# Gated mix of a state-space convolution and a routed feed-forward: parameter products ahead of the transposition, wide products, and cross-block sums by accumulating transfers

## The chip, the cores and the metric

The kernel runs on one core of one Trainium2 chip. The metric is the device time of one execution in microseconds; the time before is the median of 2 runs. Each execution can leave a profile; times inside it are counted from the start of its span.

## The reference

Input x = `A_u` has 2048 tokens of 512 channels. The output is a gated mix of two branches:

```
g   = sigmoid((x * gate_w).sum(-1))                    # per token
# branch a: state-space convolution, per channel d
A, B, C = complex (512, 128);  dt = exp(log_dt)
K[d,l]  = Re sum_n C[d,n] * exp(dt[d]*A[d,n]*l) * dt[d]*B[d,n]      # l < 2048
a   = irfft(rfft(pad(x)) * rfft(pad(K)))[:2048] + x * Dskip         # length 4096, along tokens
# branch b: the two tokens with the largest r = x @ w_r go through a feed-forward
y   = (silu(x_sel @ w_gate) * (x_sel @ w_up)) @ w_down * sigmoid(r_sel)
b   = x with y added at those two tokens
out = g * a + (1 - g) * b
```

## The kernel before, in words

The 512 channels are two halves h = 0, 1 of 256, the 2048 tokens two blocks of 1024. Every step is entered by `Prog.op` with the engine, the buffers it reads and writes and a cost; a step that may run on ACT or on DVE is given both. The order is not left to a planner at run time: the string ORDER lists all steps in the order in which each engine gets them, and SECOND says by one digit for each step whether it takes the first or the second engine named. `emit` then puts a semaphore wait ahead of a step for what it needs from another engine. So each engine works its own list in strict order, and a step that waits holds up all that stands behind it in that list. Transfers are issued by SP, or by ACT where a step says so. Most operations are entered through helpers, so their line in the profile is that of the helper: L483 is a product or sum of two tensors on DVE, L494 a function on ACT, L498 an eviction (PSUM to SBUF, on either engine), L502 a scaling for the arguments of sine and cosine, L505 a DMA.

The stages:

1. *Parameters.* A_re, A_im, C_re, C_im, B_re, B_im (four blocks of 128 channels x 128 states each) are loaded. dt is spread over the partitions by a matmul (L621) and exponentiated. 24 PE transposes (L628) bring all six to states x channels. DVE then forms AL = dt·A_re, the angle B16 from dt·A_im (L648, L651), PBR = dt·B, CM1 and CM2 (the products with C_re and C_im), and from these WW = C·B·dt in the channel order of the kernel (four small sums).
2. *Exponentials and angle tables.* 26 exponentials of AL multiples on ACT, arguments (L502, L694) on DVE or ACT, sine and cosine on ACT. The function sets of ACT differ, so a switch loads a table (L255 and the first at L494). DVE multiplies exponentials, sines and earlier tables into the rows r0 to r3 for each half (r0h to r3h; r31 is the last of half 1).
3. *Routing and feed-forward* on PE with small steps elsewhere (logits L771, gather L812, edge tokens `xed` L820, feed-forward L835, L851), and the transform of the input on PE (L900), whose evictions fill X (named x<h><block> here).
4. *kgen(h)*: 256 narrow matmuls (L917) make the kernel K of one half from the tables, evicted to KA (ka). Small selections (L933 to L966) and, for half 1, twenty small transfers on SP within SBUF (`tap`) arrange it as KC.
5. *kspec(h)*: matmuls with 128 KB spectrum matrices (L986, KP) and a cross term (L991) make the kernel's spectrum, evicted to KK (kk): for block i, real or imaginary part, quarter qd, even or odd.
6. *products(h, qds, blks)*: complex products of X and KK on DVE. Block 1 of the output needs X of block 1 with KK of block 0 plus X of block 0 with KK of block 1, so there are two further products and two additions. For block 1 of half 0 before, this is done quarter pair by quarter pair (`qd` 0, then 1), each in its own buffers PQ; block 0 is done in one wide pass in PM.
7. *inverse(h)*: per block, matmuls add the token-wise parts (`fin`, L1038, L1039) and the inverse transform with G (L1051); evictions L1059 scale by the gate into U, and a DMA writes 128 KB of output.

In the list before, half of kspec(0) (quarter pair 0) stands ahead of kgen(1) on PE and half behind it; DVE's list has products of half 0 while kgen(1) runs.

Of the kernel before, what the change touches and what calls it, by code (L numbers as in the profile page):

```python
# [58 lines left out]
class Prog:  # L59
# [47 lines left out]
    def schedule(self):  # L107
# [15 lines left out]
        dma_free = {SP: 0.0, ACT: 0.0}  # L123
# [250 lines left out]
ETB = sorted({tok(s)[0] for _, _, src in EROWS for s in src})  # L374
# [4 lines left out]
def small_mats():  # L379
    eye = np.eye(128)  # L380
    sgn = np.diag(np.where(np.arange(128) % 2 == 0, 1.0, -1.0))
    xs = np.zeros((128, len(ETB), EW))
    ek = np.zeros((128, 4, 2, EW))
    oh = np.zeros((NE, 16 * 128))
    for r, (t, k, src) in enumerate(EROWS):
        for s in src:
            tb, p = tok(s)
            xs[p, ETB.index(tb), 32 + r] = 1.0
# [4 lines left out]
    return np.concatenate([eye, sgn, -sgn, xs.reshape(128, -1), ek.reshape(128, -1)], 1), oh  # L393
# [3 lines left out]
    "00100300p00q00r00200000700o01401500601700501801c01b01p00402201e00h01d01601i01y01f01k01v01g00g01901q01j01h01x01a00802301u03u04w01n01o03t02s00a04x03v00s"  # L397
    "00t00u00v02002402d01r04303s04404200w00x00y00z01002b01s01t00c02604500901101201l01301w02102702q05903w03x03z04603y02t04704805b04z04y01m05805a04902g04005c"
    "00b02j04f05005105204a04104b05d05f02502m02i05e02u05g05h05302902o02r05502n05402p02v04n01z04e02w02l04c02a00e03304m05s03404d00i02k03502c05t03602f02e04p037"
    "03802h04g05600f02805v04o04q03903a04j05u03b03i05700d04h05w04t04i04r04s04k03d05i05k03j07807907a04l05j05l00n07l03o07s07j07b07c05y00l04u05m07r07i03e03f07t"  # L400
    "07k07m00j07e07h07q07d07u06004v07n05x05z06105n05p07g03g07o05o05q07v06207w03k03l09s06307f07p09t09h06e06f09r07x03m05r06h03n03q09u09v06g09i06506407y06609w"
    "06i06709x09j07z08108006j08309k06k06m0680820ae08508409l06906l06n08609m09o06b06a06c06d09n08908b0ad08a08e08f0a408h06z09y08c0a308808706y07003p06o08d0a1071"
    "07200k08g08i08j0ac09p0a20a508k08l08m08o08n08q0ab09z0af0a808p06q08s08r0a609q0a70a006p0a900m06r0am0al0ag08t0aa0an08u0ao07408w0b80ai0ah0ay0ax0az0ap0b508v"
    "0aj0b708y08x0aw0900b60ak08z0920au0aq0ar0at03r02x07306s06u0b00b306w0av0b90b106t0ba0bb0bc0as0be0bh0bd0b20b40bf0760bg0bj0bi0750bl0910bk0bu09306v0br09d0bq"
    "09c0bm0bp09409e0bt0bw0bs0bn0770950980bo0bv09609709a09f0c80bx09g02y0990ca06x0du0cb0c60c70c40cf0cl0cm03002z0310320er0ex0ey0cg0c50cc0by0c90f60cd0cn0f50bz"
    "0ch0f00ci0cj0ck09b0d80d90da0db0dc0ce0f70dd0de0df0f80dg0dh0di0dk0dj0dl0dm0do0dn0dq03h0dp0ds0dt03c0ei0co0f40dr0e20cp0e40f90eu0fa0fc0es0ec0fb0fe0cq0cr0ej"
    "0cs0ez0ev0ew0ct0cu0cv0c00cw0f20cx0f30cy0ff0e70d20c10e30cz0d00d10d30d40fg0eq0fd0c20c30f10d50d60ep0d70eg0fh0e90eh0fi0ek0em0en0e10el0h20h60gz0h10fj0fk0h0"
    "0dx0e60fl0ee0fm0dw0h30h50fn0h40eb0fo0ha0dy0fp0eo0hd0dv0ed0h70fq0he0hf0hp0hb0ef0h80h90hg0hn0hc0et0ho0hh0hi0hq0e50e00dz0fs0e80ea0fv0g10g20fw0fr0ft0fx0fy"
    "0fz0g60gc0g00fu0g30g70g40g50hu0gd0g80g90ga0gb0gh0gi0hj0gf0ib0gj0ge0ic0id0gg0gn0i40ie0gl0if0hr0gk0gq0gm0gr0gs0gw0go0gt0gp0hk0gu0ht0i50gv0ig0ii0ih0im0il"
    "0in0gx0gy0i10hv0i20ik0i30hs0hy0hz0i60ia0hw0jf0ij0jj0jg0i00hl0je0hx0i70jd0jk0jh0io0ip0iq0ir0is0iu0ju0it0jl0jm0jv0jn0ji0jo0iw0jw0iv0iy0jp0jq0ix0iz0i80j1"  # L410
    "0j20j30j00j70jr0js0jz0k10jt0k20k50j40j60jy0j50j80j90k30k70k40ja0jb0i90jc0k60ka0kb0k90kd0ke0kf0k00kg0kj0kk0kh0k80ki0kl0jx0kc0km0kp0hm0kq0kn0ko0kr0ks"
)
SECOND = (
    "000000000000000000000000000000000000000000000000000110000000000000000000000000000000000000000000000000000000000000000000000000000000000001110001001110"
    "000100011001010010110001001100000000010000100001000000000000000000001100000000000000000000000000000000000000001100000000001000001001000000000000000000"
    "000000000000000000000000000000000000000000000010000000101010001000001001100010100110000000000111010001101000000000000000000000000000000000000000001000"
    "000000000100000000000000000000000000000000000000000000000000000000000000000100001101100110100100000000000000000000000000000000000000000000000000000000"
    "00000000000000000000000010000110000000000000000000000000000000000000000000000000000000000000000000000000000000000000000000000000000000010110010000000"
# [5 lines left out]
def bass_gated_mix__ssm_conv_s4__moe_arch_mod__prompt_kernel(nc, A_u, A_A_re, A_A_im, A_B_re, A_B_im, A_C_re, A_C_im, A_log_dt, A_Dskip,  # L424
# [22 lines left out]
    with ExitStack() as es:  # L447
# [73 lines left out]
        CF = B("cf", oS, 640, F32); RTS = B("rts", oS + 640, 1280, F32);  # L521
# [10 lines left out]
        PBR = B("pbr", oX, 4 * KB, F32)  # L532
# [555 lines left out]
        for qd in range(2):  # L1088
            products(0, (qd,), (1,), pset=qd)
# [57 lines left out]
```

## Time and profile before

| what | us |
|---|---|
| median of 2 runs | 169.3 (169.01 to 169.58) |
| the profiled execution's own time | 168.23 |
| its span in the profile | 166.4 |
| last sine on ACT ends | 79.9 |
| last table row (r31) ends on DVE | 92.86 |
| kgen(1) on PE | 92.92 to 102.2 |
| last product ends on DVE | 159.33 |
| last output DMA issued | 164.30 |

The profiled execution is 1.83 us longer than its span; what lies around the span is not seen by the profile. Busy time is given for PE (matmul), PEld (weight load), DVE, ACT and POOL; a busy share of an engine is an average over stages, so the stages are read one by one. In the chain of waits each row is a start, a duration and the work; consecutive rows follow from what released what. In the groups of instructions, the mean is one instruction's own duration; back to back they start some 0.08 us closer than that.

### The profile page before, as it was taken

Reading aid. Unit: us, or ns where it says so; the run is one execution under the profiler, and the core shown is the slowest. Engines: PE = TensorE matmul, PEld = TensorE weight load, DVE = VectorE, ACT = ScalarE, POOL = GpSimd, SP = SyncE. Lnnn points to the kernel's source line nnn. Section 1 sums busy time; section 2 is a strip of 40 time slices with the busy share of each in tenths; the row PEclk is TensorE's granted clock in tenths of the full one; section 3 lists DMA queues with packets and bytes.
Section 4 is the critical chain, followed back from the end, with each engine's and each line's share of the span. In section 5 each row is a group of like instructions: output and inputs, shape, how many; then the busy total and the mean of one; then the engine's idle time right before and its main releaser. Section 6 shows DMA issues by size and latency. Waiting matters only on the chain.

```text
span 166.4 us, 3916 instructions
## 1 busy us (share of the span) xinstructions
PE 148.1 (89%) x1644; PEld 101.7 (61%) x1644; DVE 152.9 (92%) x255; ACT 117.2 (70%) x197; POOL 2.8 (2%) x7
## 2 busy tenths in 40 slices
PE   5999959999999998997489999968989999989980
PEld 1644415456364348692257799837857888878860
DVE  1699998899999998999999999999999999999970
ACT  3499999799999999999744777992043658408022
POOL 2000000000000000000000004000000000000000
PEclk9999987999999999999858999999999999999999
DMA  4999998996000000000995502941020000130505
GB/s 151 218 341 203 146 241 290 415 398 267 4 0 0 0 4 0 4 0 7 330 353 196 190 7 61 378 123 26 13 61 8 0 0 0 35 95 0 158 4 160
DMA packets 22584, 20.33 MB, mean 122 GB/s; under 512 B 12187, under 2 KB 19102, under 8 KB 22438
## 3 DMA queue, kind: packets, MB, share of 16 engines
q1 hardware_dynamic: 22276, 19.81, 39.7%
q8 instruction: 13, 0.21, 0.5%
q10 hardware_dynamic: 290, 0.26, 0.5%
q14 instruction: 5, 0.04, 0.1%
HBM read 15.54 MB, written 2.10 MB: 106 GB/s over the span
## 4 chain that ended last, share of the span: by engine, by line
DVE 52%; ACT 28%; PE 9%; issue 6%; DMA 2%; SPq 0%; DVEq 0%
DVE AR L483 44%; ACT AR L494 13%; ACT AR L498 7%; ACT AR L502 4%; PE ps L900 3%; ACT AR L694 3%; DVE AR L498 2%; PE ps L1051 2%; PE ps L628 2%; DVE AR L502 2%; DMA AR<-c_bf 2%; DVE AR L880 1%; PE ps L917 1%; PE ps L771 1%; DVE AR L1059 1%
## 5 line engine op out<-in xcount | busy, mean ns | idle before, releaser
L483 DVE TENSOR_TENSOR AR<-AR 128x1024 bf16<-128x1024 bf16 (+8 forms) x151 | 119.9, 839 | 1.3
L498 ACT ACTIVATE AR<-ps 128x512 bf16<-128x512 f32 (+7 forms) x71 | 45.0, 667 | 17.9 <-PE ps L986 10.2
L900 PE MATMUL ps<-AR 128*128 128x512 bf16 x192 | 45.5, 390 | 2.4 <-DVE AR L498 2.1
L494 ACT ACTIVATE AR<-AR 128x512 bf16<-128x512 f32 (+4 forms) x56 | 41.4, 791 | 2.6 <-DVE AR L483 2.2
L900 PEld LDWEIGHTS ps<-AR 128*128 128x128 bf16 x192 | 18.1, 100 | 25.4 <-DVE AR L498 2.6
L1051 PE MATMUL ps<-AR 128*128 128x256 bf16 x256 | 30.4, 273 | 1.3 <-DVE AR L483 1.3
L1051 PEld LDWEIGHTS ps<-AR 128*128 128x128 bf16 x256 | 24.8, 98 | 5.1 <-DVE AR L483 1.9
L1059 ACT ACTIVATE AR<-ps,AR 128x256 bf16<-128x256 f32 x25 | 10.8, 474 | 21.9 <-PE ps L1051 21.7
L986 PE MATMUL ps<-AR 128*128 128x256 bf16 x160 | 21.0, 282 | 0.3 <-issue 0.3
L917 PEld LDWEIGHTS ps<-AR 128*128 128x128 bf16 x512 | 18.8, 98 | 2.1 <-ACT AR L498 0.7
L917 PE MATMUL ps<-AR 128*128 128x84 bf16 (+1 forms) x512 | 19.4, 199 | 0.5 <-ACT AR L498 0.4
L986 PEld LDWEIGHTS ps<-AR 128*128 128x128 bf16 x160 | 15.5, 101 | 4.5 <-issue 0.7
L502 DVE TENSOR_SCALAR AR<-AR 128x256 int32<-128x256 f32 (+1 forms) x39 | 11.4, 325 | 0.6 <-ACT AR L494 0.6
L502 ACT ACTIVATE AR<-AR 128x256 int32<-128x256 f32 (+1 forms) x25 | 10.0, 437 | 0.0
L617 PE MATMUL ps<-AR 128*128 128x512 bf16 x28 | 8.3, 462 | 1.5 <-DVE AR L612 1.5
L1038 PE MATMUL ps<-AR 128*128 128x256 bf16 x32 | 7.7, 274 | 2.1 <-DVE AR L498 1.4
L1039 PE MATMUL ps<-AR 128*128 128x256 bf16 x32 | 7.6, 273 | 0.0
L483 DVE TENSOR_TENSOR AR<-AR,ps 128x256 f32<-128x256 bf16 (+2 forms) x6 | 3.4, 627 | 4.1 <-PE ps L628 4.1
L617 PEld LDWEIGHTS ps<-AR 128*128 128x128 bf16 x28 | 3.0, 112 | 5.4 <-issue 1.9
L991 PE MATMUL ps<-AR 128*128 128x512 bf16 x16 | 5.6, 380 | 0.1
L694 DVE TENSOR_SCALAR AR<-AR 128x1024 int32<-128x1024 int32 (+1 forms) x9 | 5.7, 629 | 0.0
L1038 PEld LDWEIGHTS ps<-AR 128*128 128x128 bf16 x32 | 3.1, 97 | 3.6 <-DVE AR L498 1.5
(66 smaller groups left out, 81.6 us busy)
## 6 DMA issues: line engine op xcount, KB each, us to landing
AR<-c_ksp SPq DMA_DIRECT2D x5, 512.0 KB, 5.5
AR<-c_inv SPq DMA_DIRECT2D x1, 2048.0 KB, 8.0
out_dram<-AR SPq DMA_DIRECT2D x16, 128.0 KB, 2.2
AR<-in_B_w_gate_dram SPq DMA_DIRECT2D x1, 1792.0 KB, 12.8
AR<-in_B_w_up_dram SPq DMA_DIRECT2D x2, 896.0 KB, 10.9
AR<-c_fwd SPq DMA_DIRECT2D x3, 512.0 KB, 6.9
AR<-in_A_u_dram SPq DMA_DIRECT2D x2, 512.0 KB, 5.3
AR<-in_A_u_dram SPq DMA_DIRECT2D x1, 1024.0 KB, 7.7
```

The lines of the kernel that those rows point to most:

```text
L483: return P.op(DVE, lambda h: h.tensor_tensor(out=o, in0=a, in1=b, op=op), rd, wr, cost=tt_cost(o, a, b), **k)
L494: return P.op(ACT, lambda h: h.activation(out=o, in_=a, func=func, scale=scale, bias=bias), rd, wr, cost=0.185 + nel(o) * 0.833e-3 + (0.09 ...
L498: return P.op((ACT, DVE), (lambda h: h.activation(out=o, in_=a, func=ACTF.Copy), lambda h: h.tensor_copy(o, a)), rd, wr, cost=(0.185 + n * ...
L502: return P.op((ACT, DVE), (lambda h: h.activation(out=o, in_=a, func=ACTF.Copy, scale=c), lambda h: h.tensor_scalar(out=o, in0=a, scalar1= ...
L617: last = h.matmul(fwp[1](0, 128, k * 512, (1, D)), DUM(0, 128, 0, (1, 128)), DUM(0, 128, 0, (1, D)), start=True, stop=True)
L694: P.op((DVE, ACT), (lambda hh: hh.tensor_scalar(out=w, in0=w, scalar1=16384.0, scalar2=None, op0=ALU.add), lambda hh: hh.activation(out=w, ...
L900: last = h.matmul(o, w, U2(0, 128, st * D, (1, D)) if pm else U(0, 128, (blk * 8 + st * 2 + par) * D, (1, D)), start=(pm + par + st == 0), ...
L917: last = hh.matmul(pb(0, 128, (g - b0) * W4 + o, (1, n)), TP[h][1 - i // 2](0, 128, g * 128, (1, 128)), r[i](0, 128, g * n, (1, n)), start ...
L986: last = hh.matmul(pb(0, 128, n * 256, (1, 256)), KP[u](0, 128, (tau + n) * 128, (1, 128)), KC[h](0, 128, jg * 256, (1, 256)), start=(k == ...
L1038: hh.matmul(pb(0, 128, e * 256, (1, 256)), IDN(0, (1, 128)), U(0, 128, tb[e] * D + h * HC, (1, HC)), start=(e == 0), stop=False)
L1051: last = hh.matmul(pb(0, 128, e * 256, (1, 256)), G(0, 128, ((par * 2 + part) * 4 + ft) * 512 + (2 * t2 + e) * 128, (1, 128)), X(0, 128, h ...
L1059: P.op((ACT, DVE), (lambda hh, o=o, i_=i_, g_=g_: hh.activation(out=o, in_=i_, func=ACTF.Copy, scale=g_), lambda hh, o=o, i_=i_, g_=g_: hh ...
```

## The change

- *Parameters.* A_re and A_im alone are brought over by 8 matmuls with a permuted identity, so they come out in the kernel's channel order at once; dt is spread in that order too. C and B are multiplied on DVE in their natural layout (PAB, bf16), and 16 accumulating matmuls (identity and negated identity NID) both transpose the products and add them up to C·B; WW is one product with dt. B_im is issued on ACT behind the exponential of dt in ACT's list.
- *Edge tokens.* Two row loads bring the few token rows (XSR), and one matmul with a selection matrix takes the place of four.
- *Taps of half 1.* Every second one is issued by ACT. The load of G stands behind the SP ones.
- *Block 1 of half 0* is one pass over both quarter pairs. Its two cross products go to PT and to X's own block-1 place, and are added to PM by POOL: two groups, each of two DMAs of 128 x 2048 bf16 with `accum_op=ADD`.
- *Outputs* are grouped by pairs of token tiles of the same parity; still 16 of 128 KB.
- *Order.* New ORDER and SECOND: all 26 exponentials come before the first sine; all of kspec(0) stands behind kgen(1) on PE; in DVE's list, four ka evictions of half 1, eight kk evictions of half 0 and two wide products come between r31 and the first cross product; then u scalings, kc1's addition, the second cross product, eleven steps of half 1 (kk1 evictions and products of quarter pair 0), and behind them the subtraction that needs both accumulated buffers. DVE takes more evictions than before, ACT fewer. kspec(1) stands ahead of inverse(0).

```diff
-        dtp = kgp[1]
-        pps = [misb[0], misb[1], kgb[0]]
...
-                        last = h.transpose(pps[q](0, 128, i * D + k * 128, (1, 128)), PRM(0, 128, (2 * q + i) * D + k * 128, (1, 128)), IDN(0, (1, 128)))
+        TS(NID(0, 128, 0, (1, 128)), IDN(0, (1, 128)), -1.0, ALU.mult, [CBI], [NID])
...
+                    last = h.matmul(pto(psa[q], 0, k), PRM(0, 128, q * D + k * 128, (1, 128)), idp(CB, 0), start=True, stop=True)
+        for q in range(2):
+            TT(PAB(0, 128, q * 1024, (D, 2), (1, D)), PRM(0, 128, 2 * D, (D, 2), (1, D)), PRM(0, 128, (4 + q) * D, (0, 2), (1, D)), ALU.mult, [(PRM, 2), (PRM, 3), (PRM, 4 + q)], [(PAB, q)])
+        for part in range(2):
+            def pwr(h, part=part):
+                for k in range(4):
+                    h.matmul(pto(psw, part * D, k), PAB(0, 128, part * D + k * 128, (1, 128)), idp(CB, 0), start=True, stop=False)
+                    last = h.matmul(pto(psw, part * D, k), PAB(0, 128, 1024 + (1 - part) * D + k * 128, (1, 128)), idp(CB, 0) if part else idp(NID, 0), start=False, stop=True)
...
+        TT(f512(AL), f512(DTB), psa[0](0, 128, 0, (1, D)), ALU.mult, [DTB, psa[0].buf], [AL])
+        STT(f512(TMP[1]), psa[1](0, 128, 0, (1, D)), -c16, f512(DTB), ALU.mult, ALU.mult, [DTB, psa[1].buf], [TMP[1]])
...
-        TT(PBR(0, 128, 0, (D, 2), (128, 4), (1, 128)), DTB(0, 128, 0, (0, 2), (1, 4), (4, 128)), pps[2](0, 128, 0, (D, 2), (128, 4), (1, 128)), ALU.mult, [DTB, pps[2].buf], [PBR])
-        TT(c2(CM1), pps[1](0, 128, 0, (D, 2), (1, D)), PBR(0, 128, 0, (0, 2), (1, D)), ALU.mult, [pps[1].buf, PBR], [CM1])
-        TT(c2(CM2), pps[1](0, 128, 0, (D, 2), (1, D)), PBR(0, 128, D, (0, 2), (1, D)), ALU.mult, [pps[1].buf, PBR], [CM2])
-        for h_ in range(2):
-            TT(prd(WW, 0, h_), tra(CM1, 0, h_), tra(CM2, D, h_), ALU.subtract, [CM1, CM2], [(WW, (0, h_))])
-            TT(prd(WW, D, h_), tra(CM1, D, h_), tra(CM2, 0, h_), ALU.add, [CM1, CM2], [(WW, (1, h_))])
+        TT(WW(0, 128, 0, (D, 2), (1, D)), DTB(0, 128, 0, (0, 2), (1, D)), psw(0, 128, 0, (D, 2), (1, D)), ALU.mult, [DTB, psw.buf], [(WW, (p_, h_)) for p_ in range(2) for h_ in range(2)])
...
+                return h.matmul(xe(0, EW, 0, (1, D)), CB(0, len(ESRC), ECOL, (1, EW)), XSR(0, len(ESRC), 0, (1, D)), start=True, stop=True)
...
-                    DMA([(KC[h](32 * k, 32, ...), kd(...))], [KA[h]], [(KC[h], (u0, k, c4))], 60000 * nu, prio=1e5, each=0.6)
+                    DMA([(KC[h](32 * k, 32, ...), kd(...))], [KA[h]], [(KC[h], (u0, k, c4))], 60000 * nu, prio=1e5, each=0.6, eng=(SP, ACT)[c4 % 2])
...
+            if blks == (1,) and len(fts) == 4:
+                for qd in qds:
+                    xq = X(0, 128, h * 8192 + 4096 + 512 * qd, (2048, 2), (1024, 2), (1, 512))
+                    for P_, part in ((PA, 0), (PBb, 1)):
+                        kq = KK[h](0, 128, part * 2048 + 512 * qd, (0, 2), (1024, 2), (1, 512))
+                        TT(P_(0, 128, 512 * qd, (2048, 2), (1024, 2), (1, 512)), xq, kq, MUL, [...], [(P_, ('q', qd))])
...
+                if blk == 1 and len(fts) == 4:
+                    for P_, part in ((PA, 0), (PBb, 1)):
+                        t_, tk = (v4(PT), [PT]) if part else (xv(1), kx(1))
+                        TT(t_, xv(0), kv(1, part), MUL, kx(0) + kk(1, part), tk)
+                        src = (lambda c: PT(0, 128, c, (1, 2048))) if part else (lambda c: X(0, 128, xo(1, 0, 0) + c, (1, 2048)))
+                        P.op(POOL, lambda hh, P_=P_, src=src: [hh.dma_start(P_(0, 128, 2048 * i, (1, 2048)), src(2048 * i), accum_op=ADD) for i in range(2)], tk, [P_], cost=2.0, n=2, nbytes=2500000, dma=True)
...
-        for qd in range(2):
-            products(0, (qd,), (1,), pset=qd)
+        products(0, (0, 1), (1,))
         products(0, (0, 1), (0,))
```

More of the change, by code (lines that the diff above doesn't have):

```diff
@@ L122, in schedule @@
         free = {e: 0.0 for e in ENGS}
-        dma_free = {SP: 0.0, ACT: 0.0}
+        dma_free = {SP: 0.0, ACT: 0.0, POOL: 0.0}
         ndep = [len(o.deps) for o in ops]
@@ L399 @@
[L399 to L406, printed above, removed]
@@ L759, in routing @@
         def routing():
+            for t0 in (0, BLK):
+                ts = [t for t in ESRC if t0 <= t < t0 + BLK]
+                assert ts == list(range(t0, t0 + len(ts)))
+                DMA([(XSR(ESRC.index(t0), len(ts), 0, (1, D)), dr(A_u, t0 * D, (D, len(ts)), (1, D)))], [], [(XSR, t0)], 4096)
             for db in range(4):
```

105 lines of the change are left out of this document (55 added, 50 removed).

## The prediction

> **What bounds the kernel now.** I read four views in this order: the page, the chain of waits, the timeline around the late stage, and the groups by shape. The page first, with its busy tenths in 40 slices of 4.16 us:
>
> ```profile
> PE 148.1 (89%) x1644; PEld 101.7 (61%) x1644; DVE 152.9 (92%) x255; ACT 117.2 (70%) x197; POOL 2.8 (2%) x7
> DVE  1699998899999998999999999999999999999970
> ACT  3499999799999999999744777992043658408022
> DVE 52%; ACT 28%; PE 9%; issue 6%; DMA 2%; SPq 0%; DVEq 0%
> ```
>
> DVE is full from the third slice to the last but one, ACT only up to the nineteenth. The chain of waits says the same by stages: on DVE at first, on ACT from 30.91 to 79.9, then on DVE.
>
> ```profile
> 30.91 1.28 ACT L255
> 32.20 2.10 ACT AR L494 x2
> ...
> 78.01 1.90 ACT AR L494 x2
> ...
> 82.44 10.42 DVE AR L483 x12
> ...
> 126.61 4.63 DVE AR L483 x4
> ...
> 159.05 3.25 PE ps L1051 x28
> ```
>
> So three stages are to be costed: ACT's sines (the chain runs over a table load and the L494 activations up to 79.91), DVE's last table rows (r31, end 92.86), and DVE's 66.5 us from there to the last product at 159.33. After that product 7.07 us follow (inverse, eviction, output) to the span of 166.4. The timeline shows what surrounds r31:
>
> ```profile
> 86.17 5.17 PE L986 MATMUL ps<-AR 128*128 128x256 bf16 x36
> 92.92 9.28 PE L917 MATMUL ps<-AR 128*128 128x84 bf16 x256
> 102.03 3.65 PE L986 MATMUL ps<-AR 128*128 128x256 bf16 x32
> 105.87 11.53 SPq L505 DMA_DIRECT2D AR<-AR  x17
> ```
>
> Half of half 0's kernel spectrum (L986) is made on PE before kgen(1) (L917), the rest after it. So DVE has half-0 products to do while PE spends 9.28 us in kgen(1).
>
> **The change, part by part.** Durations below are start to start in unbroken runs, about 0.08 us under the means in these rows:
>
> ```profile
> L483 DVE TENSOR_TENSOR AR<-AR 128x2048 bf16<-128x2048 bf16 x48 | 57.5, 1220 | 0.4
> L483 DVE TENSOR_TENSOR AR<-AR 128x1024 bf16<-128x1024 bf16 x44 | 29.2, 687 | 0.4
> L483 DVE TENSOR_TENSOR AR<-AR 128x4096 bf16<-128x4096 bf16 x2 | 4.5, 2285 | 0.0
> ```
>
> That is 1.14, 0.60 and 2.20 us.
>
> *Parameters.* DVE loses four 256-wide products at 0.50, three 1024-wide f32 at 1.13, one L648 at 0.33 and four f32 combinations at 0.52: 7.8. It gains two 1024-wide bf16 at 0.60, one 1.13, two 512-wide PSUM operations at about 0.60 and a negation at 0.13: 3.7. Net -4.1 on DVE. The first product waits for A_re alone (landing in 2.8) and 4 matmuls, not 8 transposes of 1.03 us per eight: AL starts at about 4.6 (before 5.57), the first exponential at 5.25 (6.70). C x B needs B_im, which ACT now issues behind the dt exponential; 2.9 us later it lands at about 7.3, which costs DVE 0.5 of standing, counted in the stalls below. The 16 accumulating matmuls lie on PE, which only warms up there: 0, at most the 1.03 of a row of eight.
>
> *Exponentials before sines.* Before has four table loads of 1.28, after two: -2.56 on ACT. From first exponential to last sine the work on ACT is 66.3 before and 66.6 after (five more arguments, two evictions fewer), without loads; before took 73.2 (3.84 loads, 3.0 idle). After: 5.25 + 66.6 + 1.28 = 73.1 with no idle, 76.1 with the old idle; I take 74.7. r31 ended 12.96 behind the last sine; the rows left to do are nearly the same (13.5), so r31 ends at about 88.2 (bounds 86.1 to 89.6). Gain 4.7. DVE's own work to that point fell more (84.8 to 78.4), but it would then stand some 5.2 us waiting for exponentials and sines; ACT sets the end.
>
> *Spectrum of half 0 wholly behind kgen(1).* Now PE needs, from r31 on: 9.3 for kgen(1), then up to the last spectrum group that the wide product needs 76 matmuls at 0.114 (3.65/32) and 6 cross terms of 0.22, 10.0 us, and one eviction of 0.6 (L498). The wide product can start at 88.2 + 19.9 = about 108.1. On DVE's list between r31 and it stand 5.6 us (gates, u scalings, four kgen evictions, one early eviction) and 7.2 us (eight spectrum evictions at 0.60, two wide products at 1.14, small ones): 12.8. So DVE stands about 7.1 us, a hole that was not there. The cover that would hide this cost, half-0 products during kgen(1), is exactly what the order gives up.
>
> *Wide products and cross-block sums.* Before: 12 of 2048 and 8 of 1024, 13.7 + 4.8 = 18.5. After: 8 of 2048 and 2 of 4096, 9.1 + 4.4 = 13.5. DVE -5.0, four additions of them (4.6) given to POOL's two transfer groups, each 2 x 512 KB added into SBUF.
>
> *Evictions.* In all DVE's list goes from 149.1 to 145.8 (hand sum), ACT's from 105.4 to 102.4: of the 9.1 saved on DVE, 5.8 are taken back by evictions moved from ACT. From r31 to the last product DVE's work is 62.3 before, 66.1 after.
>
> *The accumulating transfers.* No row of before has one. They are issued at about 110.4 (behind the first wide product) and 116.4. The subtraction that needs both stands behind 10.1 us of kk1 evictions and half-1 products, and so starts at about 127. Low bound 6.7 to 7.7 us per MB (w_down, u: 1024 KB), high 15.4 (twice the u row, since the destination is read as well), or 30.8 from the first issue if the second queues behind the first. I take 8.0, the row of 2 MB (c_inv), since each group reads two MB and writes one: lands at 124.4, hidden with 2.7 to spare. [...]
>
> *Queues.* Ten of the twenty tap transfers go from SP (11.53/17 = 0.68 each) to ACT, which issues them between spectrum evictions: about 6.5 us of ACT in a stretch (98 to 110) where ACT has only 8 of evictions and scalings. Taken as 0, bounds -1 (taps land earlier, kc1's addition no longer waits; before stood 1.9 at 118.3) to +2 (an eviction that PE waits for stands behind issues). The 2 MB c_inv moves behind SP's ten taps, to about 105, lands about 113, is needed at about 129: 0. The two row loads for the edge tokens (which turn four matmuls of L820 into one) and the regrouped outputs (still 16 x 128 KB): 0; the first lie far ahead of their use in a stage that ACT bounds, and the last outputs are still released by the last evictions.
>
> *Sum.* 88.2 + 66.1 work + 7.1 hole + 2.4 of smaller waits (before 4.2) = 163.8 for the last product; before 159.33. Tail 7.07 as before: span about 170.9 against 166.4, +4.5. The profiled execution took 168.23, 1.07 under the median of 169.3; 169.3 + 4.5 = 173.8.
>
> **The rivals.** *(A) The transfers outlast their cover.* If the second group lands later than 127, DVE stands at the subtraction. [...] For it: no row prices an addition in flight, and four 512 KB transfers share the engines with the end of c_inv. Against: 10.7 us of cover against 8.0.
>
> *(B) No change.* r31 ends at its early bound, 86.1 (-2.1), and taps and spectra come without waits (-2.4): 169.3. For it: four places of the chain where "issue" stood 0.8 to 1.9 us are tap and spectrum waits. Half of this, 171.5, is already within 2%.
>
> *(C) Faster, by one mechanism: the hole does not open.* If kgen(1) and the spectrum ran so that DVE's 12.8 us filled the time from r31 to the wide product, 7.1 would go: 166.7; with half of B's waits 165.5. It decides for faster when the last spectrum eviction comes 7.9 us sooner than 108.1, at 100.2. Against it: kgen(1) needs r31, 256 matmuls took 9.28 us at a granted clock of 1.00, and 76 more cannot follow in 2.7. Only a far earlier r31 (80.3) could do the same, and DVE's 78.4 us of work from 4.6 on forbid it.
>
> **How the numbers follow.** About 2% (3.4 us: 165.9, 172.7) is what a measurement of this kernel can tell from no change. Forecast 0.42, 173.8, own range 171 to 176.5; A 0.22 (176.5 to 188); B 0.28 (168.5 to 172); C 0.08 (164 to 166.5). Slower: A and three quarters and more of the forecast, 0.58; faster: C and little else, 0.08; same 0.34. The range leaves out C and half of B's lower end below, A's far end above: 168 to 180.
>
> **What would show it.** Right: first exponential at 5.2 to 5.5 and a single table load after the first, at about 19; r31's end near 88; DVE idle some 7 us between r31 and the wide product, released by PE L917, L986 and their evictions; chain through PE in 88 to 108; DVE starting the subtraction without a wait on POOL's transfers; last product to end 7.1. Wrong: r31 before 86 or after 90, DVE busy over 90% in 88 to 108, or a wait of DVE on a DMA at about 127.

## The result and the profile after

The changed kernel takes 180.1 us (median of 2 runs, 179.91 to 180.29) against 169.3: a ratio of 1.064, 95% interval 1.057 to 1.071. It is slower, as forecast, but by 10.8 us and not by 4.5. In the profiled executions the span went from 166.4 to 178.4. Here and below the ratio leaves disturbed executions out and the median doesn't, so where the two differ the ratio is used; the profiles of the kernels with ratios 1.082 and 1.115 are of disturbed executions, and times from them are rough.

The page of the changed kernel, the lines that answer to those shown of before:

```profile
PE 153.4 (86%) x1628; PEld 103.2 (58%) x1642; DVE 150.4 (84%) x246; ACT 111.7 (63%) x188; POOL 6.4 (4%) x11
DVE  1565999999999999999946698963999999999940
PEclk9999999559999999999999999557999999999998
DVE 34%; PE 33%; ACT 21%; DMA 6%; issue 3%; SPq 0%; DVEq 0%
```

DVE, full before from the third slice on, now has a gap in slices 21 to 28, from 89 to 125 us. In the chain PE's share rose from 9% to 33%. PE's granted clock dips to 0.50 twice, from 30.39 to 40.63 and from 112.31 to 122.55 us. Before had two shorter dips to 0.50, 3.41 us from 23.53 on and 6.83 from 81.55 on, both ahead of r31:

```profile
PEclk9999987999999999999858999999999999999999
```

The chain of waits around the gap:

```profile
90.10 6.49 PE ps L920 x177
...
97.22 2.95 PE ps L920 x79
100.17 3.80 PE ps L989 x34
...
110.23 7.59 DMA AR<-AR
117.84 0.29 DVE AR L482
...
118.30 4.86 PE ps L989 x24
```

From 88 on it runs over PE (kgen(1), then all of kspec(0)), as forecast. Then come two things that were not: 7.59 us of one small transfer within SBUF, a tap, and behind it kspec(1), whose 24 matmuls take 4.86 us at a mean clock of 0.56 (at the 0.114 each that they took before at a clock of 1.00, it would be 2.7). The timeline of DVE, only the rows with idle time ahead of them (in brackets, with what ended it), gives the sizes:

```profile
90.16 0.42 DVE L497 CAST AR<-ps 128x256 bf16<-128x256 f32 x1 [0.82 <-PE ps L948]
93.65 0.68 DVE L497 CAST AR<-ps 128x504 bf16<-128x504 f32 x1 [1.55 <-PE ps L920]
...
99.65 1.10 DVE L497 CAST AR<-ps 128x504 bf16<-128x504 f32 x2 [3.06 <-PE ps L920]
...
107.40 0.69 DVE L497 CAST AR<-ps 128x512 bf16<-128x512 f32 x1 [0.54 <-PE ps L989]
117.84 0.28 DVE L482 TENSOR_TENSOR AR<-AR 1x256 bf16<-1x256 bf16 x1 [1.43 <-DMA AR<-AR]
123.88 2.36 DVE L482 TENSOR_TENSOR AR<-AR 128x2048 bf16<-128x2048 bf16 x2 [2.69 <-ACT AR L497]
```

With two of 0.18 that are left out, 6.3 us for PE's kgen(1) and spectrum, 1.4 for the tap, 2.7 for the spectrum of half 1. Before had no such row behind r31. The windows from r31's end to the end of the last product (us, then busy time of PE, PEld, DVE, ACT and POOL, with instructions, then clock, DMA share and GB/s), of before:

```profile
92.86:159.33 66.47, 61.74 (x768) 52.59 (x768) 65.28 (x88) 34.55 (x68) 1.85 (x1) 1.00 0.24 72
```

and of the changed kernel:

```profile
89.34:170.66 81.32, 70.42 (x816) 57.78 (x819) 69.80 (x94) 32.12 (x59) 5.44 (x5) 0.94 0.40 113
```

So the 12.0 us of span are: r31 3.5 sooner (92.86 to 89.34), DVE 4.5 more to do behind it (65.3 to 69.8), 10.3 more of DVE not busy (1.2 to 11.5), tail 0.7 longer (7.07 to 7.74).

### The profile page after: what moved, and what is told of

Same layout as the page of the kernel before. It is cut to its first block, busy times and chain, and to the rows that moved or that the text cites. A ratio compares the mean times of both kernels' runs of the same rounds, so it can differ in the third digit from the quotient of the medians.

```text
span 178.4 us, 3883 instructions
## 1 busy us (share of the span) xinstructions
PE 153.4 (86%) x1628; PEld 103.2 (58%) x1642; DVE 150.4 (84%) x246; ACT 111.7 (63%) x188; POOL 6.4 (4%) x11
## 4 chain that ended last, share of the span: by engine, by line
DVE 34%; PE 33%; ACT 21%; DMA 6%; issue 3%; SPq 0%; DVEq 0%
DVE AR L482 29%; ACT AR L493 8%; PE ps L989 8%; ACT AR L497 8%; PE ps L903 7%; PE ps L920 5%; DMA AR<-AR 4%; ACT AR L501 4%; PE ps L616 4%; PE ps L1066 2%; DVE AR L501 2%; DMA AR<-in_A_A_re_dram 2%; PE ps L936 1%; ACT AR L696 1%; DVE AR L1074 1%
## 5 line engine op out<-in xcount | busy, mean ns | idle before, releaser
L482 DVE TENSOR_TENSOR AR<-AR 128x1024 bf16<-128x1024 bf16 (+6 forms) x139 | 113.5, 866 | 8.1 <-ACT AR L497 2.7
L497 ACT ACTIVATE AR<-ps 128x512 bf16<-128x512 f32 (+5 forms) x58 | 39.8, 704 | 34.0 <-PE ps L989 13.9
L903 PE MATMUL ps<-AR 128*128 128x512 bf16 x183 | 44.8, 393 | 1.5 <-ACT AR L497 0.6
L903 PEld LDWEIGHTS ps<-AR 128*128 128x128 bf16 x192 | 18.1, 101 | 24.0 <-ACT AR L497 3.0
L1066 PE MATMUL ps<-AR 128*128 128x256 bf16 x256 | 29.9, 273 | 1.2 <-DVE AR L482 1.1
L1066 PEld LDWEIGHTS ps<-AR 128*128 128x128 bf16 x256 | 24.8, 98 | 4.8 <-DVE AR L482 2.0
L989 PE MATMUL ps<-AR 128*128 128x256 bf16 x160 | 22.8, 295 | 4.8 <-ACT AR L497 2.8
L989 PEld LDWEIGHTS ps<-AR 128*128 128x128 bf16 x160 | 16.0, 105 | 10.5 <-ACT AR L497 3.7
L920 PEld LDWEIGHTS ps<-AR 128*128 128x128 bf16 x512 | 18.8, 98 | 3.1 <-ACT AR L497 1.4
L497 DVE CAST AR<-ps 128x512 bf16<-128x512 f32 (+5 forms) x19 | 13.4, 719 | 6.5 <-PE ps L920 4.8
L501 ACT ACTIVATE AR<-AR 128x256 int32<-128x256 f32 (+1 forms) x31 | 13.0, 449 | 0.1
L616 PE MATMUL ps<-AR 128*128 128x512 bf16 x27 | 9.0, 490 | 1.6 <-DVE AR L611 1.5
L501 DVE TENSOR_SCALAR AR<-AR 128x256 int32<-128x256 f32 (+1 forms) x33 | 10.1, 334 | 0.2
L1053 PE MATMUL ps<-AR 128*128 128x256 bf16 x32 | 7.6, 273 | 1.7 <-ACT AR L497 1.7
L1054 PE MATMUL ps<-AR 128*128 128x256 bf16 x32 | 7.6, 272 | 0.0
L616 PEld LDWEIGHTS ps<-AR 128*128 128x128 bf16 x28 | 3.1, 117 | 5.9 <-issue 2.8
L883 ACT ACTIVATE AR<-AR 128x512 bf16<-128x512 bf16 x8 | 5.6, 710 | 0.0
L870 POOL MEMSET AR<- 128x2048 bf16 x1 | 1.8, 1809 | 98.7 <-PE ps L920 98.7
```

Source lines behind the costliest of these rows:

```text
L482: return P.op(DVE, lambda h: h.tensor_tensor(out=o, in0=a, in1=b, op=op), rd, wr, cost=tt_cost(o, a, b), **k)
L497: return P.op((ACT, DVE), (lambda h: h.activation(out=o, in_=a, func=ACTF.Copy), lambda h: h.tensor_copy(o, a)), rd, wr, cost=(0.185 + n * ...
L501: return P.op((ACT, DVE), (lambda h: h.activation(out=o, in_=a, func=ACTF.Copy, scale=c), lambda h: h.tensor_scalar(out=o, in0=a, scalar1= ...
L616: last = h.matmul(fwp[1](0, 128, k * 512, (1, D)), DUM(0, 128, 0, (1, 128)), DUM(0, 128, 0, (1, D)), start=True, stop=True)
L903: last = h.matmul(o, w, U2(0, 128, st * D, (1, D)) if pm else U(0, 128, (blk * 8 + st * 2 + par) * D, (1, D)), start=(pm + par + st == 0), ...
L920: last = hh.matmul(pb(0, 128, (g - b0) * W4 + o, (1, n)), TP[h][1 - i // 2](0, 128, g * 128, (1, 128)), r[i](0, 128, g * n, (1, n)), start ...
```

## The experiments

All are edits of the changed kernel or of the one before, timed beside the one before. `mv(E, [i], F, j)` in the diffs puts entry i of engine E's list into F's list ahead of its entry j, counted in the changed kernel. Where a diff names whole lists, ORDER and SECOND were put together anew in that way.

**The taps, the wait behind them, and G.** First the load of G (c_inv) put off:

```diff
-DMA([(G(0, 128, 0, (1, 8192)), g_c[:, :])], [], [G], 2097152)
+DMA([(G(0, 128, 0, (1, 8192)), g_c[:, :])], [(KC[1], (0, 0, 0))], [G], 2097152)
```

> The changed kernel, with the 2 MB load of G (c_inv) waiting for kc1's addition, so that it is issued behind the taps' landing. Theory T (two taps, issued last by ACT at 110.2 to 111.6, stood behind the 2 MB load issued on SP at 109.0 and landed only at 117.8): taps land by about 114, DVE's wait of 1.43 before kc1's addition goes, the spectrum of half 1 starts some 3.5 earlier, the wait of 2.69 for kk1 shrinks below 1: 176.5 to 178. Rival A (the accumulating transfers, issued at 113.5, held the taps): the wait stays, 179.5 to 180.5.

Measured: 179.74, ratio 1.064 (1.058 to 1.070): no gain, the expectation missed. The tap no longer held DVE (its row with 1.43 is gone, so it had indeed stood behind the 2 MB), but kc1's addition came at 116.9 in place of 117.8 all the same, behind DVE's own products, the wait for kspec(1) stayed at 1.81, and G, now issued at 117.2, ran beside the transfers of POOL. These took 11.6 us to land (6.7 in the changed kernel), and DVE waited 0.78 for them at 133.87; no row of PE waits for G. The next kernel took the two late taps from ACT and left G:

```diff
+mv(ACT, [145, 146], SP, 50)   # last two taps of ACT: SP, ahead of G
```

> The changed kernel, with the last two taps taken from ACT's list to SP's, ahead of G. Theory T: SP issues them at about 109.0 to 110.3, they land at about 113, G follows at 110.3 and lands at about 119: the waits of 1.43 and most of 2.69 go, 176.5 to 178. Rival A: taps still land with the transfers, 179.5 to 180.5.

Measured: 179.03, ratio 1.059 (1.053 to 1.065): 1.1 us better, less than the theory's number. The tap's wait is gone here too, the one for kspec(1) still 2.14. What was left was DVE's own order: the addition that completes kc1 stood behind products of 2.3 us each, and PE, which needs it, stood.

```diff
+mv(ACT, [145, 146], SP, 50)
+mv(DVE, [185], DVE, 181)      # kc1's addition ahead of block 0's wide products
```

> As e2 (last two taps on SP ahead of G), and kc1's addition moved on DVE from behind the products of PM0 to ahead of them. Theory H (PE stood for kc1's addition long enough to fall to half clock, and made the spectrum of half 1 at half pace, so that kk1 came late): kspec(1) starts about 2.3 earlier than in e2 (113.2 in place of 115.5), the half clock goes or shortens, DVE's wait of 2.1 for kk1 goes: 176 to 177.5 against 179.0 for e2. Rival (the wait for kk1 is the evictions' own pace): 178.5 to 179.5.

Measured: 177.15, ratio 1.047 (1.041 to 1.053), 3.0 us under the changed kernel: the theory's number. The window of 110 to 120 in the changed kernel:

```profile
110.00:120.00 10.00, 5.98 (x83) 4.14 (x83) 8.46 (x13) 2.35 (x4) 1.89 (x2) 0.62 0.99 292
```

and in this one:

```profile
110.00:120.00 10.00, 8.07 (x106) 6.28 (x106) 9.20 (x14) 3.80 (x7) 1.89 (x2) 0.83 0.83 250
```

PE's clock there is 0.83 in place of 0.62, DVE's waits of 1.43 and 2.69 are gone (one of 0.70 is new). The theory's mechanism is only half borne out: kspec(1) started at 115.23 and not at 113.2, and the half clock was not brought on by the stand for kc1's addition. In the changed kernel PE stood twice, and the clock was already half ahead of the second stand, the one for the tap:

```profile
113.35 0.58 PE L862 MATMUL ps<-AR 128*2 128x128 bf16 x4 [1.78 <-DVE AR L497]
118.30 5.93 PE L989 MATMUL ps<-AR 128*128 128x256 bf16 x34 [1.89 <-DVE AR L482]
```

```profile
112.50:116.40 3.90, 2.69 (x17) 1.44 (x18) 3.90 (x8) 0.81 (x2) 1.89 (x2) 0.50 0.97 390
```

The first stand, for a small eviction behind the first wide product, is there in all these kernels, and the half clock behind it too: from 112.31 to 122.55 in the changed kernel, 113.29 to 120.11 with the taps moved, 114.61 to 118.02 here. That is 10.24, 6.82 and 3.41 us, or three, two and one times 3.41. Counted in stretches of 3.41, each kernel's last stretch is the first in which PE did not stand: the tap's stand ends at 118.30, in the second of three; with the taps moved PE stood 1.08 for kc1's addition until 115.52, in the first of two; here it does not stand again. So the tap's stand did not start the slow clock, which began 4.1 us ahead of it (112.31 and 116.41). That it drew the slow clock out is my reading of these three traces; no run shows how. Stand and longer slow clock are together about 3 us, in time gained by the two moves.

**The transfers.** The additions back on DVE:

```diff
-P.op(POOL, ... [hh.dma_start(..., accum_op=ADD) for i in range(2)], tk, [P_], ...)
+TT(v4(P_), v4(P_), t_, ADD, tk + [P_], [P_])
```

> The changed kernel, with the two cross-block sums as two DVE additions of 4096 (2.20 each, where POOL issued them before) in place of the accumulating transfers. Theory T: DVE gets 4.4 more, of which up to 2.7 falls into its wait for kk1 at 121.2: 181 to 183. Rival A (the transfers slow what goes on around them): the waits of DVE at 116 to 124 shrink with them, 176 to 179.

Measured: 181.76, ratio 1.077 (1.070 to 1.084), 1.7 us slower than the changed kernel: the theory's number. The transfers save time, but some 1.7 of the 4.6 us that the two additions take (the two intervals touch, so the size is rough). Rival A falls: with them no row of DVE waits for POOL's queue, and the page has them landing in

```profile
AR<-AR POOLq DMA_DIRECT2D x4, 512.0 KB, 6.7
```

**The lists of before and after, by halves.** Lists of the changed kernel up to r31, behind it the steps and lists of before (half the spectrum ahead of kgen(1), quarter-pair products, additions on DVE, all taps on SP):

```diff
 ORDER, SECOND up to r31: as changed
-products(0, (0, 1), (1,))
+for qd in range(2):
+    products(0, (qd,), (1,), pset=qd)
```

> The changed kernel up to r31 (parameters, edge tokens, exponentials first, its lists on every engine up to there), and behind it the steps and lists of the kernel before (two passes for block 1, additions on DVE, taps on SP, old outputs). Theory T (the loss lies behind r31, in the lists there; but with the new early lists PE ends the transform some 9 us later, so half 0's spectrum matrices land at about 95 and its first half falls behind r31 anyway): r31 at 89 to 90, DVE stands some 6 to 9 us before the first product: 171 to 175. Rival B (the late lists alone are to blame, the early part keeps its 3.5): 165 to 167.

Measured: 177.32, ratio 1.048 (1.043 to 1.054): above both numbers, though the stand before the first product is as the theory had it. r31 ends at 88.7, 4.2 us sooner than before, and all of it is lost at once. DVE's timeline, then PE's:

```profile
99.85 2.36 DVE L482 TENSOR_TENSOR AR<-AR 128x2048 bf16<-128x2048 bf16 x2 [9.47 <-ACT AR L497]
```

```profile
93.56 5.57 PE L989 MATMUL ps<-AR 128*128 128x256 bf16 x36 [2.46 <-DMA AR<-c_ksp]
```

The changed lists end PE's input transform (L903) 8 to 10 us later than before (87.6 in the changed kernel, 85.7 here, 78.0 before), so the spectrum matrices c_ksp are loaded later (issued from 85.77; before from 78.03), and the half of the spectrum that should stand ahead of kgen(1) starts at 93.56 (before 86.17). r31's gain was bought with work put off on PE.

The other half, lists of before up to r31 (with the new parameter step), behind it as changed:

```diff
 ORDER, SECOND up to r31: as before, with the new parameter operations
 behind r31: as changed
```

> The opposite: the lists of the kernel before up to r31 (exponentials and sines mixed; the parameter step is the new one), and the changed kernel's steps and lists behind it. Theory T: r31 ends at 91.5 to 93, PE stands about 8 us before it, and from r31 on all goes as in the changed kernel, 80.7 to the last product: 181 to 184. Rival C (PE's delay and half clock in the early stage cause the loss): with PE on time 170 to 174.

Measured: 183.28, ratio 1.082 (1.073 to 1.090), the theory's number. Some 3.6 of it lie ahead of r31 (96.44; before 92.86, and 91.5 to 93 expected), since DVE stands 6.96 us at 16.45 for PE's parameter matmuls. From r31 to the last product it takes 80.4, about what the changed kernel takes (81.3): the late part by itself brings the loss behind r31. In this kernel and the next one the load of G stands ahead of SP's taps. The next kernel takes half the spectrum ahead of kgen(1) again:

```diff
 lists of the last kernel, and:
+kspec(0) of quarter pair 0 ahead of kgen(1) on PE, its evictions on ACT
+two wide products directly behind r31
 taps: ten still on ACT
```

> As e8, but the first half of kspec(0) stands ahead of kgen(1) on PE, where PE would stand, its evictions on ACT, and the two wide products that need only it stand in DVE's list behind r31; the last two taps are on SP. Theory T (the hole is kgen(1) and all of kspec(0) in a row): 4 to 7 faster than e8: 175 to 178. Rival (DVE is held by its own work, the hole only moves): within 1.5 of e8.

Measured: 182.13, ratio 1.078 (1.071 to 1.085), 1.2 us less: the theory's number is missed, the rival's met. The kernel that ran differs from what was expected of it in one thing: the last two taps were not moved, ACT issues ten as in the changed kernel. kgen(1) was filled, but nine of these taps (0.69 us each, from 105.7 to 111.9) now stood in ACT's list ahead of evictions that PE waits for:

```profile
112.60 0.61 PE L989 MATMUL ps<-AR 128*128 128x256 bf16 x2 [3.63 <-ACT AR L497]
```

**One more try at the early lists.** The input transform brought forward on PE:

```diff
+mv(SP, [22], SP, 27)           # w_gate behind c_fwd
+mv(PE, [32, 34, 35], PE, 40)   # three routing steps behind 12 transform matmuls
```

> The changed kernel, with w_gate loaded behind the last two transform matrices on SP, and PE's routing matmuls L802, L818 and the first L838 moved behind 12 transform matmuls, so that PE does not stand from 27.0 to 31.9 and keep the halved clock until 40. Theory T (the loss lies behind r31, whose end DVE sets): the transform ends 6 to 9 us earlier on PE, r31's end stays within 1 us of 89.3, kgen(1) starts at it and not 0.8 later: 178 to 179.8. Rival B (PE's 9 us of delay are what the chain of waits of 72 to 110 shows, and the cause of the loss): 171 to 175.

Measured: 189.92, ratio 1.115 (1.105 to 1.125): both numbers missed. The lists interlock:

```profile
36.95 3.57 PE L903 MATMUL ps<-AR 128*128 128x512 bf16 x8 [9.60 <-ACT AR L497]
```

PE waited 9.6 us for an eviction that stood in ACT's list behind work that waited for the steps moved. It says nothing on the theories.

**The parameter step alone.** Everything as before (four table loads, old order), with the new step, its 16 matmuls ahead of five of PE's warm-ups (`warm` in the kernel, matmuls on a constant buffer whose results nothing reads):

```diff
 ORDER, SECOND: as before; parameter operations as changed
+PE: ptr, ptr, five warm-ups, pwr, pwr, WL's transposition, five warm-ups
```

> The kernel before in everything but the parameter step, which is the new one (products ahead of the transposition, its 16 accumulating matmuls put ahead of five of the warm-up matmuls); four table loads, half the spectrum ahead of kgen(1), additions on DVE, all taps on SP as before. Theory (the parameter step is good, the order behind r31 loses what it gains; ACT sets r31's end, so only the earlier first exponential counts, 1.4 us and a little of DVE's standing): 166.0 to 168.2. Rival (the parameter step itself loses, since its matmuls and the late load of B_im hold DVE): 169.5 to 172.

Measured: 169.77, ratio 1.006 (1.003 to 1.009), within 2%: the rival's number. r31 ends at 93.8, 1.0 later than before; DVE stands 4.27 at 13.75 for WL's transposition, which waits behind the 16 matmuls. Earlier still:

```diff
-PE: ptr, ptr, five warm-ups, pwr, pwr, WL's transposition, five warm-ups
+PE: ptr, ptr, two warm-ups, WL's transposition, pwr, pwr, eight warm-ups
```

> The kernel before with the new parameter step alone (169.77 us), with the transposition for WL ahead of the 16 accumulating matmuls, and both ahead of eight warm-ups instead of five. Theory (16 accumulating matmuls of 0.22 us, 3.5 in all, were priced at 0 to 1 and hold WL and WW; ACT then stood 2.04 at its second table load for arguments queued on DVE behind WL): that stand goes, r31 1 to 2 us sooner, 167.6 to 168.8. Rival (the same ACT work with four table loads sets r31 whatever comes early): 169.3 to 170.2.

Measured: 170.68, ratio 1.009 (1.005 to 1.014): a little over even the rival's number. r31 ends at 92.7, as before, though the first exponential starts at 5.86 (6.70 before). PE and ACT in this kernel:

```profile
17.48 10.09 PE L903 MATMUL ps<-AR 128*128 128x512 bf16 x45
```

```profile
24.59 1.02 ACT L497 ACTIVATE AR<-ps 128x1024 bf16<-128x1024 f32 x1 [2.23 <-PE ps L903]
```

The transform starts 3.6 us later than before (13.90), and ACT stands for it. In the changed kernel PE's early rows are

```profile
5.63 6.59 PE L616 MATMUL ps<-AR 128*128 128x512 bf16 x20
12.06 0.38 PE L641 MATMUL ps<-AR 128*128 128x128 bf16 x1
12.26 0.40 PE L642 MATMUL ps<-AR 128*128 128x128 bf16 x1
...
15.67 0.17 PE L650 MATMUL ps<-AR 8*128 8x8 bf16 x1
```

so 16 matmuls take 3.6 us, 0.22 each, where a transposition of the kernel before took 0.13 (3.14 for 24). In the second parameter kernel DVE's lighter list (3.5 us less busy in the first 30 us than before) turns into standing.

**The hole behind r31.** A light spectrum, which leaves out two of four terms of each of half 0's groups:

```diff
-uses = [u for u, (bi, jg) in enumerate(KUSE) if bi == i]
+uses = [u for u, (bi, jg) in enumerate(KUSE) if bi == i][:None if h else 2]
```

> As the kernel with the last two taps on SP and the kc1 addition ahead of the products (177.15 us), but of half 0's spectrum groups each leaves out two of its four matmul terms, 32 of 80 matmuls of 0.114 us, so the output isn't the reference's. Theory (PE sets the time from r31 to the wide product): 3.65 us less in that stretch, 173.0 to 174.5. Rival (DVE's own work and the evictions set it, PE's time there is slack): 176.3 to 177.4.

Measured: ratio 1.043 (1.035 to 1.051) against 1.047 (1.041 to 1.053): no difference shown; the theory's number is missed, the rival's met. With 3.65 us less on PE, r31 to the wide product took 20.4 us instead of 21.5, and DVE was 9.54 of 10 us busy in 100 to 110 (9.03 with the full spectrum). So most of the hole lies in kgen(1), where DVE's list has nothing for it; behind that DVE's own evictions and products pace it, not the matmuls. Then the wide form with the cover given back, on the lists of before, with c_inv ahead of the taps. As in the last run of the lists by halves, the taps stayed by turns on SP and ACT, though the expectation has them all on SP:

```diff
 up to r31: the first parameter kernel above
 behind r31: wide products and transfers as changed, but
+kspec(0) of quarter pair 0 ahead of kgen(1); two wide products behind r31
+taps behind G, ten of them still on ACT; kc1's addition ahead of the products
```

> As the kernel with the parameter step alone (first run of this call) up to r31, and with half the spectrum ahead of kgen(1), all taps on SP, c_inv ahead of them as in the kernel before; but half 0's block 1 is made by the wide products and the accumulating transfers, two of its four first products right behind r31, the kc1 addition ahead of the products, as the changed kernel behind that. Theory (not the wide form but the spectrum wholly behind kgen(1) costs the time): within 3 us of the first run of this call, 166 to 170. Rival (the wide form itself costs it, since its second factor needs both quarters of the block-1 spectrum, which come late on PE whatever goes first): 173 to 177.

Measured: 178.29, ratio 1.052 (1.044 to 1.060); on the rival's side, a little over its number. The profiled execution is the shortest of four (176.08; the others 178.2 to 178.6). The windows from r31 to the last product, of the first parameter kernel and of this one:

```profile
93.82:160.47 66.65, 61.54 (x764) 52.54 (x768) 65.28 (x89) 33.87 (x66) 1.85 (x1) 1.00 0.23 71
```

```profile
93.44:166.85 73.41, 62.13 (x754) 52.22 (x759) 64.87 (x88) 30.22 (x56) 5.45 (x5) 0.98 0.36 90
```

73.4 is 7.9 less than the changed kernel's 81.3, so the lists are worth that much of this stretch; but it is 6.8 more than with products by quarter pairs, at the same work of DVE. DVE's rows with waits:

```profile
102.35 1.10 DVE L497 CAST AR<-ps 128x504 bf16<-128x504 f32 x2 [3.43 <-PE ps L920]
...
109.52 2.29 DVE L482 TENSOR_TENSOR AR<-AR 128x4096 bf16<-128x4096 bf16 x1 [1.35 <-ACT AR L497]
...
114.44 1.41 DVE L482 TENSOR_TENSOR AR<-AR 1x256 bf16<-1x256 bf16 x2 [2.03 <-DMA AR<-AR]
```

The taps have a part in the last two: ACT issues five in a row, PE waits for the eviction behind them, and the wide product for what PE makes then.

```profile
104.28 3.48 ACTq L504 DMA_DIRECT2D AR<-AR  x5
108.47 0.39 PE L994 MATMUL ps<-AR 128*128 128x512 bf16 x1 [1.49 <-ACT AR L497]
```

A pass over both quarter pairs can start its second half of products only when all of block 1's spectrum is there; before, the first pair's whole chain of products fills kgen(1). That the wide form costs some of the 6.8 by itself is the plainest reading, but it is not shown: the wait of 2.03 is the taps', the 1.35 at least in part.

**Transfers in the old order.** On the second parameter kernel, the first pair's two additions in half 1's block 1 by transfers of 512 KB:

```diff
-TT(xv(1), xv(0), kv(1, part), MUL, ...); TT(v4(P_), v4(P_), xv(1), ADD, ...)
+TT(pq if part else xv(1), xv(0), kv(1, part), MUL, ...)
+P.op(POOL, lambda ...: [hh.dma_start(v4(P_), pq if part else xv(1), accum_op=ADD)], ...)
```

> As the second run of this call, with one more part of the change alone: the two additions of half 1's block 1, first quarter pair, on DVE (2 x 1.14 us), made by accumulating transfers of 512 KB from POOL, their consumers put behind the second pair's products. Theory (behind r31 DVE waits for PE's spectrum as soon as it has less to do, so work taken from it turns into standing, and what is put off for the transfers comes on top): 1 to 4 us slower than that run. Rival (DVE is 98% busy there, so it is 2.3 us faster).

Measured: 176.47, ratio 1.044 (1.036 to 1.051), 5.8 us slower than that kernel. DVE's rows with waits that the kernel without them lacks, one of PE's, and the window of 140 to 150:

```profile
135.41 1.23 DVE L482 TENSOR_TENSOR AR<-AR 128x2048 bf16<-128x2048 bf16 x1 [1.04 <-ACT AR L497]
138.72 23.29 DVE L482 TENSOR_TENSOR AR<-AR 128x2048 bf16<-128x2048 bf16 x32 [2.09 <-ACT AR L497]
```

```profile
150.83 1.89 PE L1071 MATMUL ps<-AR 128*128 128x256 bf16 x8 [5.58 <-DVE AR L482]
```

```profile
140.00:150.00 10.00, 5.25 (x47) 4.29 (x44) 9.72 (x11) 4.81 (x11) 0.00 (x0) 0.91 0.43 101
```

DVE stands 3.1 us for the spectrum of half 1 as soon as it has less to do. The products put off for the transfers then come late for the inverse: PE stands 5.58 for them, is 5.25 us busy where the kernel without them had 9.19, and its clock is 0.80 from 150 to 162.5 (1.00 without them). DVE's last product ends at 162.0, 1.4 later, and 12.6 us follow it (7.4 without them), most of them PE's. Theory's direction, a size beyond it.

**The tail and a best version.** Two evictions back to DVE, the parameter matmuls earlier:

```diff
 taps and kc1 as above, and:
+mv(PE, [14, 15, 16], PE, 9)    # pwr, pwr and WL's transposition ahead of five warm-ups
+mv(ACT, [196, 198], DVE, end)  # two of the last evictions
```

> As the kernel with the last two taps on SP and the kc1 addition ahead of the products (177.15 us), with the accumulating parameter matmuls ahead of five warm-up matmuls, and two of the last six output evictions given back from ACT to DVE. Theory (the 1.8 us wait for WL and B x C in the first 16 us sets part of r31's end; the four evictions of 0.47 in a row set the tail): r31 0.5 to 1.5 sooner, tail 0.9 shorter, 174.7 to 175.8. Rival (ACT's chain of exponentials sets r31 and absorbs the first): tail alone, 176.2 to 176.6.

Measured: 176.19, ratio 1.042 (1.035 to 1.049): between the two numbers, next to the rival's. r31 at 88.3, 1.1 sooner, as the theory had it; the tail, which the theory had 0.9 shorter, stayed at 7.9 (7.8). Then the order of the last products:

```diff
+mv(DVE, [239, 240, 241, 243], DVE, 234)   # third frequency tile ahead of the fourth
+mv(PE, [215, 217, 219], PE, 214)
```

> As the kernel with the taps on SP, the kc1 addition early, the accumulating parameter matmuls ahead of five warm-ups and two last evictions on DVE (176.19 us), with DVE's last products in another order: the third frequency tile's whole set ahead of the fourth's, and PE's inverse matmuls of the third ahead of the fourth's in the same way. Theory (the tail is 1.3 longer because the two tiles' products end together, so 40 matmuls of 0.114 us are left behind the last product instead of 28): some 16 to 24 left, tail 1.5 to 2.5 shorter, 173.7 to 174.9. Rival (the tail hangs on evictions and outputs, not on that order): 175.7 to 176.7.

Measured: 178.11, ratio 1.053 (1.045 to 1.060): no gain; this theory falls. PE's timeline and its window:

```profile
165.01 5.40 PE L1066 MATMUL ps<-AR 128*128 128x256 bf16 x48
```

```profile
160.00:170.00 10.00, 10.00 (x94) 8.96 (x92) 7.32 (x16) 2.97 (x7) 0.00 (x0) 1.00 0.29 80
```

PE doesn't stand at all from 160 to 170: it works off what was left over earlier, by the stands and the slow clock in the middle (0.83 from 110 to 120, 0.86 and 0.80 in the two windows of ten behind it) as I read it. No version here beats the kernel before; the nearest, the parameter step alone, is level with it.

## Why the prediction was right in its sign and wrong in its size

The terms of the sum against the spans: r31 +1.1 (89.34 for 88.2), r31 to the last product +5.7 (81.3 for 75.6), tail +0.7 (7.74 for 7.07), together 7.5 of span. What lies around the span was 0.3 shorter (1.51 for 1.83) and the median 0.9 nearer to the profiled execution, so 6.3 of median, 180.1 for 173.8.

- *What bounds.* Right, with one thing missing: PE, too, was 61.7 of 66.5 us busy behind r31. I read only DVE's 65.3. Where a run took work from DVE there (the transfers in the old order, two additions less), DVE stood 3.1 us for PE's spectrum instead.
- *Parameters.* DVE's relief was right (4.1 forecast; in all 152.9 us busy before, 149.0 and 149.4 in the two parameter kernels). The 16 accumulating matmuls on PE, taken as "0, at most the 1.03", failed: they took 3.6 us, behind 20 warm-ups. WL's copy waits 1.8 at 15.9, B_im holds DVE 1.4 (0.5 forecast), and the first exponential starts at 5.77, not 5.25. Moving the matmuls gave r31 1.1, as much as the whole error of that term.
- *Exponentials before sines.* Right in size (one load at 19.4 behind the first; 19 forecast), and r31 within its bounds. But the gain came from the lists, not from the parameter step, which alone put r31 1.0 us later, and 0.2 sooner in its second form; and the price, PE's transform 9.6 us later (87.6 for 78.0), was not in the sum as such.
- *Spectrum behind kgen(1).* The hole was forecast as 7.1 and measured as 6.3, in the right place. Its reason was half right: the light spectrum, 3.65 us less on PE for 1.1 us less of the stretch, shows that the matmuls behind kgen(1) set little of it.
- *DVE's work behind r31.* Nearly right: +3.8 forecast, +4.5 measured.
- *Smaller waits, 2.4.* Wrong: without the tap's and the spectrum's they stayed at 4.1 (before 4.2), 1.7 more than I took, and I had no reason for less.
- *Queues.* "Taken as 0, bounds -1 to +2": this is the step that failed most. The last two taps, issued by ACT at 110.2 behind an eviction, came after c_inv (109.0, not 105) and took 7.6 us where such a transfer took 1.8 to 3.0. DVE stood 1.4 for the tap and 2.7 for kspec(1) behind it, which ran at a mean clock of 0.56: 4.1 where the sum had 0. The bound of +2 held for the tap alone; the slow clock on PE, which began 4.1 us ahead of that stand and lasted 10.24 us, against 6.82 in the kernel without it, was not thought of. Taking the two taps from ACT gave back 1.1 us, and with kc1's addition earlier in DVE's list 3.0.
- *Transfers.* Right that they are hidden: 6.7 us to land for each 512 KB against 8.0 taken for a group, no wait. That is no fixed price: they took 9.6 us in the run with kc1's addition early, 11.6 in the one with G late, where DVE did wait 0.78, and 5.8 in the old order with two of them. POOL issued 0.3 us behind the product it waited for, both times, and took 1.89 and 1.74 us for two.
- *Tail as before.* 0.7 short. Neither the side of the last evictions nor the order of the last products was the cause. PE has 40 matmuls left behind the last product where it had 28 before:

```profile
170.04 4.54 PE L1066 MATMUL ps<-AR 128*128 128x256 bf16 x40 [0.45 <-DVE AR L482]
```

The kernels with the late lists of before, transfers left aside, have 28 and tails of 7.1 to 7.4; those with the changed ones that keep the order of the last products have 40 and 7.7 to 7.9. But no run took this backlog alone away, so that it is the cause is argued and not shown.
- *Rivals.* A fell (no wait at the subtraction, which started at 134.2). Its 176.5 to 188 were added up from an estimate of 15.4 us a group, side by side or one behind the other, which no run shows: each 512 KB took 6.7 us, and 11.6 with G late. B and C did not come: r31 missed B's early bound by 3.2 us, and the hole of C opened.

What stays open: how much of the 6.8 us of the wide form is its own, and how much the lists into which it was put and the ten taps left on ACT; and why the clock fell at 112.31, 0.7 us into a stand.

## What to carry to other kernels

Cost each moved step on every engine's list, also on one that seems to have nothing else to do, and see which engine is next: here PE was at 93% behind DVE's 98%, and when 2.3 us of additions were taken from DVE it stood 3.1 us for PE. When two variants differ in order, ask what the earlier end of one stage put off: r31 came 3.5 us sooner, and in the same lists PE's transform ended 9.6 later. A small transfer that something waits for should be issued ahead of a large one, not beside it from another queue: here such a tap took 7.6 us beside 2 MB, where the taps on the page of the changed kernel had medians of 1.8 to 3.0, and with the two taps issued ahead of the 2 MB the wait of 1.43 for them was gone.

## What was not expected of the hardware

- A 128x128 matmul with the permuted identity, written to a permuted output, took 0.22 us start to start (8 in 1.92, and the 16 of the parameters), a plain transposition 0.13. Which of the differences between them costs the time, no run shows.
- A tap of 4 to 20 KB issued by ACT at 110.23, 1.2 us behind SP's 2 MB, took 7.6 us, though the two had different issuers. The 2 MB, issued at 109.01, took 8.6 us, so they landed at 117.6 and 117.8.
- PE stood 4.9 us from 26.99 on, and its clock was half from 30.39 to 40.63; it was half again from 112.31 to 122.55, though PE had worked until 111.6 (the last 1.55 us on 56 matmuls of two columns). The first drop came 3.4 us into a stand, the second 0.7 us into one, and no run here shows why.
- The half clock lasted 10.24 us twice in the changed kernel, 3.41 and 6.83 in the one before: three, one and two times 3.41. In eight of the runs a window of ten us has a clock of 0.83, as 3.41 us at half clock would give. The two drops of the changed kernel are 81.92 us apart, 24 times 3.413. Why, no run shows. Behind the wide product it lasted 10.24 us in the changed kernel, where PE stood 1.89 us for the tap, 6.82 in the next, where it stood 1.08, and 3.41 in the last, where it did not. From 30 to 40 the clock was 0.52 though PE was 7.6 us busy.
